# Rest q and k loaded for four heads per transfer set instead of two, with the load, transpose and v order of the second batch rearranged

## The chip, the cores and the metric

The kernel runs on one core of one Trainium2 chip. The metric is the device time of one execution in microseconds (us), lower is better. A core has five engines that run their own instruction streams and meet at semaphores: TensorE (PE, matmuls, with a separate row PEld for its weight loads), VectorE (DVE), ScalarE (ACT), GpSimd (POOL) and SyncE (SP). SP computes nothing here: it issues DMA transfers, one after the other, in program order. POOL issues transfers too, between its own computations. A transfer runs on its own once it is issued, and the instruction that needs the data waits for its semaphore.

## What is computed

Eight batches of eight heads of causal attention with a forgetting gate, then a two-layer MLP over the 4,608 tokens:

```python
batch, n_heads, seq, head_dim = (8, 8, 576, 64)

scores = np.matmul(q, k.transpose(0, 1, 3, 2)) / np.sqrt(D)
cum = np.cumsum(np.log(np.clip(f, 0.0001, 1.0)), axis=-1)
scores = np.where(causal, -1e9, scores + cum[:, :, :, None] - cum[:, :, None, :])
attn = np.exp(scores - max); attn = attn / (attn.sum(-1) + 1e-9)
x = np.matmul(attn, v).transpose(0, 2, 1, 3).reshape(4608, 512)
h = x @ w_in            # 512 -> 2048
out = (h / (1 + np.exp(-h))) @ w_out   # 2048 -> 512
```

## The kernel before

**Tiling.** A head's 576 tokens are cut into a first block of 128, three "rest" blocks of 128 (tokens 128 to 511), and a tail of 64. The first blocks of all batches have a path of their own at the start of the program. The rest works in **units**: unit n is two heads of batch n // 4, and with p = n % 4 these are heads `head(p, 0)` and `head(p, 1)` (L149): 0 and 2 for p = 0, 1 and 3 for p = 1, 4 and 6 for p = 2, 5 and 7 for p = 3. So units 2m and 2m + 1 share heads 0 to 3 or 4 to 7. There are 32 units, in 16 pairs m.

**The life of a unit.** These steps of one unit are named throughout:

- `load_qk` (L152, transfers at L158): SP loads q and k of the rest blocks into the staging tiles `qf` and `kf`. One transfer for each of q and k and each of the two heads, four in all, of 96 KB each. Four staging buffers of each.
- `load_tails` (L165, L168): the tails of all eight heads of a batch, one transfer for q and one for k, 128 KB each.
- `cast_qk` (L394): POOL turns them into bf16 in the tile `qkb`: two casts of 128x384 (L399, for q and k) and one of 128x128 (L403, tails).
- `transposes` (L423, L427): SP issues one DMA transpose from `qkb` to `qkT`. There are three `qkT` buffers, so the transpose of unit n also waits until the scores of unit n - 3 are done.
- `scores` (L444, L459): PE multiplies from `qkT`, in three pieces c = 0, 1, 2; ACT takes the exponential (L463, L475), DVE masks.
- `load_v` (L174, L179): SP loads v of a batch, one transfer for each of the blocks c = 0 to 3 (256 KB, the last one 128 KB), into one buffer for each block. `convert_v` (L409, L413): POOL multiplies it by the decay weights into `vp`, the operand of the second attention product.
- `attend` (L490): PE multiplies the exponentials by `vp` (L506, L515), DVE divides. `back` (L531) transposes the result into the MLP's input: on PE for the first pairs, by two DMA transposes on SP (L538, L542) for pairs 4 to 14.

**The MLP** is cut into small pieces (`m1_chunk`, L567, L575, L576, and `m2_part`, L612, L622). They are laid between the attention steps by a planner: `fill` and `slot` (L698, L863) put about so many microseconds of MLP matmuls at a place, by a fixed cost for each piece. The planner knows nothing of transfers. The output's stores (L591) are issued by POOL at fixed places of its own stream.

**Order.** Every engine's instructions run in the order in which the program writes them. There is no scheduler: a place in the Python text is a place in the queue. Two places set the order of the loads:

- The start (L783 to L803): load units 0, 1 and 2, then cast and transpose them, with `load_v(0, ...)`, `load_qk(3)` and `load_tails(1)` between, then `convert_v(0, ...)`.
- `prepare(n)` (L839), called once for each unit while unit n's scores are under way: it loads unit n + 4, and casts and transposes unit n + 2. Below is the part that matters; `b, p = divmod(n, 4)`.

```python
        if n > 1 and n + 4 < NU:
            load_qk(n + 4)
        if 0 < n < NU - 2:
            cast_qk(n + 2)
            transposes(n + 2)
        if n <= 1:
            load_qk(n + 4)
        ...
        if p == (1 if b > 0 else 2):
            for c in range(NM):
                load_v(b + 1, c)
```

For each pair m the main loop (L872) writes scores of unit 2m, pieces 0 and 1; `prepare(2m)`; `back(m - 1)`; MLP; scores of 2m, piece 2, and of 2m + 1, piece 0; `prepare(2m + 1)`; MLP; the other scores; MLP; then both `attend`.

Of the kernel before, what the change touches and what calls it, by code (L numbers as in the profile page):

```python
# [10 lines left out]
FP32 = mybir.dt.float32  # L11
BF16 = mybir.dt.bfloat16
P = 128
# [5 lines left out]
def kernel(  # L19
# [12 lines left out]
    B, H, S, D = q.shape  # L32
# [4 lines left out]
    NP = H // 2  # L37
    SM = 512
    ST = S - SM
    NM = SM // P  # L40
    NR = NM - 1
# [3 lines left out]
    NU = B * NP  # L45
    NQ = NU // 2
# [10 lines left out]
    stage = ctx.enter_context(tc.tile_pool(name="stage", bufs=1))  # L57
# [91 lines left out]
    def head(p, i):  # L149
        return p // 2 * 4 + 2 * i + p % 2  # L150

    def load_qk(n):  # L152
        b, p = divmod(n, NP)
        ts = []
        for name, src in (("qf", q), ("kf", k)):
            t = stage.tile([P, NR, 2, D], FP32, name=name, tag=name, bufs=4)
            for i in range(2):
                nc.sync.dma_start(  # L158
                    out=t[:, :, i, :],
                    in_=src[b, head(p, i), P:SM, :].rearrange("(c p) d -> p c d", p=P),  # L160
                )
            ts.append(t)
        qst[n] = tuple(ts)

    def load_tails(b):  # L165
        t = stage.tile([P, H, D], FP32, name="qktf", tag="qktf", bufs=2)
        for i, src in enumerate((q, k)):
            nc.sync.dma_start(  # L168
                out=t[i * ST : (i + 1) * ST, :, :],
                in_=src[b, :, SM:S, :].rearrange("h s d -> s h d"),  # L170
            )
        tst[b] = t

    def load_v(b, c):  # L174
        if c == 0:
            vst[b] = []
        t = vfs[c]
        r = slice(0, P) if c < NR else slice(ST, P)
        nc.sync.dma_start(  # L179
            out=t[r, :, 0:D],  # L180
            in_=v[b, :, P + c * P : min(S, P + (c + 1) * P), :].rearrange("h p d -> p h d"),
        )
        vst[b].append(t)
# [36 lines left out]
    for i in range(2):  # L220
        for g in range(2):
            nc.vector.tensor_copy(
                out=sel[:, i, :].rearrange("p (u w r) -> p u w r", u=2, w=2)[:, g, :, :],
                in_=ident_bf[:, :].rearrange("p (r u i w) -> p u i w r", u=2, i=2, w=2)[
                    :, g, i, :, :
                ],
            )

    def keep_warm(n):
# [7 lines left out]
        out=f_sb[:, :], in0=f_sb[:, :], scalar1=1e-4, scalar2=1.0, op0=ALU.max, op1=ALU.min  # L237
# [101 lines left out]
    def convert_v0(b):  # L339
        nc.gpsimd.tensor_tensor(  # L340
            out=v0[b][:, :, :],
            in0=vf0.pop(b)[:, :, :],
            in1=w_bf[:, 0, b * H : (b + 1) * H, None].to_broadcast([P, H, D + 1]),
            op=ALU.mult,
        )
# [48 lines left out]
    def cast_qk(n):  # L394
        b, p = divmod(n, NP)
        t2 = conv.tile([P, NX, 2 * D], BF16, name="qkb", tag="qkb")
        for i, t in enumerate(qst.pop(n)):
            c0 = i * (NR + 1)
            nc.gpsimd.tensor_copy(  # L399
                out=t2[:, c0 : c0 + NR, :].rearrange("p c x -> p (c x)"),  # L400
                in_=t[:, :, :, :].rearrange("p c h d -> p (c h d)"),
            )
        nc.gpsimd.tensor_copy(  # L403
            out=t2[:, NR, :].rearrange("s (i d) -> s i d", i=2),
            in_=tst[b].rearrange("s (u i w) d -> s u w i d", u=2, w=2)[:, p // 2, p % 2, :, :],
        )
        qbf[n] = t2

    def convert_v(b, c):  # L409
        vbf[b] = vps[b % 2]  # L410
        r = slice(0, P) if c < NR else slice(ST, P)
        n = r.stop - r.start
        nc.gpsimd.tensor_tensor(  # L413
            out=vbf[b][r, c, :, :],
            in0=vst[b][c][r, :, :],
            in1=w_bf[r, c + 1, b * H : (b + 1) * H, None].to_broadcast([n, H, D + 1]),
            op=ALU.mult,
        )
# [4 lines left out]
    def transposes(n):  # L423
        src = qbf.pop(n)
        t = qktp.tile([P, NX, P], BF16, name="qkT", tag="qkT")
        qkT[n] = t[:, :, :].rearrange("p x c -> p (x c)")
        nc.sync.dma_start_transpose(  # L427
            out=t[:, :, :], in_=src[:, :, :].rearrange("p x c -> p (x c)")
        )
# [352 lines left out]
    load_v0(7)  # L782
    after(w_out_bf[0:1, 2 * NFC // WQ - 1, DM - 16 : DM])  # L783
    load_qk(0)
    load_tails(0)
    load_qk(1)
    load_qk(2)
    cast_qk(0)
    transposes(0)
    convert_v0(6)  # L790
    convert_v0(7)
    load_v(0, 0)
    load_v(0, 1)
    cast_qk(1)
    transposes(1)
    load_v(0, 2)
    load_v(0, 3)
    load_qk(3)
    cast_qk(2)
    transposes(2)  # L800
    load_tails(1)
# [37 lines left out]
    def prepare(n):  # L839

        b, p = divmod(n, NP)
        if n > 1 and n + 4 < NU:
            load_qk(n + 4)
        if 0 < n < NU - 2:
            cast_qk(n + 2)
            transposes(n + 2)
        if n <= 1:
            load_qk(n + 4)
        if b + 1 == B:
            return  # L850
        if p == 0 and b > 0:
            load_tails(b + 1)
        if p == (1 if b > 0 else 2):
            for c in range(NM):
                load_v(b + 1, c)
        if p >= 2:
            for c in range(2 * (p - 2), 2 * (p - 1)) if b > 0 else range(NM * (p - 2)):
                convert_v(b + 1, c)
# [13 lines left out]
    for m in range(NQ):  # L872
        n = 2 * m
        piece = 1.7 if m < 2 else 2.4
        scores(n, 0)
        scores(n, 1)
        prepare(n)
        if m > 0:
            back(m - 1)
            if m % 2 == 0:  # L880
                b = m // 2 - 1
                pending.append([2, [REST_OF[b]] + ([TAILS_OF[b][0]] if b == NM - 1 else [])])
        slot(piece, 1, 0)
        scores(n, 2)
        scores(n + 1, 0)
        prepare(n + 1)
        slot(piece, 1, 0)
        scores(n + 1, 1)
        scores(n + 1, 2)
        slot(piece, 1, 0)  # L890
        attend(n)
        attend(n + 1)
        slot(min(3.5, max(0.8, behind() - LAG)) if m > 1 else 0.8)
# [38 lines left out]
```

## Time and profile before

| | us |
|---|---|
| median of 10 runs (345.59 to 350.22) | 347.68 |
| the profiled execution | 347.87 |
| its span in the trace | 346.1 |
| TensorE busy | 336.6 |
| ScalarE busy | 217.1 |
| VectorE busy | 180.4 |
| GpSimd busy | 127.5 |
| transfers of qf and of kf, 64 each of 96 KB: median from issue to landing | 3.0 and 3.2 |
| transfers of vf by SP, 26 of 256 KB: the same | 4.8 |
| transposes to qkT, 32: the same | 4.0 |

The span is the stretch between the first and the last instruction on the core; the execution's own time is 1.77 us longer. "Busy" is the time in which an engine has an instruction under way. PE's matmuls overlap each other, so the mean duration of one is more than the step from one to the next. An engine's rows in the timeline give the start, the length, the engine, the line and operation, and in brackets how long the engine had been idle before and which event ended that idle time. Rows of SPq are issues: their length is how long SP was occupied with issuing, and the data land later.

### The profile page before, as it was taken

To read this page: it belongs to the slowest core of one execution; us is meant where nothing else is said; L and a number is where in the kernel's file an instruction comes from. 1 tells how busy PE (TensorE), PEld (TensorE's weight loads), DVE (VectorE), ACT (ScalarE), POOL (GpSimd) and SP (SyncE) were. 2 spreads that over 40 slices of the span, in tenths; PEclk is the share of its full clock that TensorE was granted. 3 is DMA by queue.
4 is the path that set the end of the run, shared out by engine and by line. 5 is a ranking of instruction groups with operands and counts; after the bars stand their busy time and mean duration, and the time that the engine had idled before them with its cause. 6 is when DMAs were issued, how large, how long until landed. Compare 5 with 4: busy or idle time off the path is not lost.

```text
span 346.1 us, 8894 instructions
## 1 busy us (share of the span) xinstructions
PE 336.6 (97%) x3567; PEld 199.4 (58%) x3567; DVE 180.4 (52%) x389; ACT 217.1 (63%) x401; POOL 127.5 (37%) x227
## 2 busy tenths in 40 slices
PE   8999999998899999999999999999999999999995
PEld 3654655666466566466555666656656565555654
DVE  4756736367167566446545545555655454344330
ACT  5866644886457857759558686685776844454431
POOL 8986226734545083065045108208320000001011
PEclk9999999999899999999999999999999999999999
DMA  8999999999999998999798799989622010001012
GB/s 154 196 186 219 192 182 148 245 207 179 202 215 194 155 209 170 158 226 171 131 233 152 146 184 171 179 168 207 135 67 73 5 60 35 30 31 62 30 50 73
DMA packets 141497, 50.44 MB, mean 146 GB/s; under 512 B 132368, under 2 KB 138768, under 8 KB 141456
## 3 DMA queue, kind: packets, MB, share of 16 engines
q1 hardware_dynamic: 131440, 32.70, 56.0%
q0 software_dynamic: 9856, 17.04, 21.2%
q8 instruction: 28, 0.46, 0.6%
q10 hardware_dynamic: 160, 0.13, 0.2%
q14 instruction: 13, 0.11, 0.1%
HBM read 36.85 MB, written 9.44 MB: 134 GB/s over the span
## 4 chain that ended last, share of the span: by engine, by line
PE 85%; DMA 7%; POOL 2%; SPq 2%; ACT 1%; DVE 1%; issue 1%; POOLq 0%
PE po L612 35%; PE hp L567 33%; PE sc L459 6%; PE dn L506 4%; PE dn L515 2%; DMA w_in_bf<-in_moe_w_in_dram 2%; DMA vf<-in_v_dram 2%; PE tp L285 1%; DMA qkb<-in_k_dram 1%; DMA qkT<-qkb 1%; SPq L427 1%; DMA kf<-in_k_dram 1%; DVE gt L576 1%; SPq L158 1%; POOL vf L140 1%
## 5 line engine op out<-in xcount | busy, mean ns | idle before, releaser
L576 DVE SCALAR_TENSOR_TENSOR gt<-th,hp 128x384 bf16<-128x384 bf16 (+2 forms) x208 | 105.7, 522 | 83.8 <-ACT th L575 79.8
L575 ACT ACTIVATE th<-hp 128x384 bf16<-128x384 f32 (+2 forms) x208 | 95.2, 478 | 84.7 <-PE hp L567 82.4
L612 PE MATMUL po<-w_out_bf,gt 128*128 128x512 bf16 (+1 forms) x592 | 146.1, 376 | 0.0
L567 PE MATMUL hp<-x,w_in_bf 128*128 128x384 bf16 (+2 forms) x704 | 128.5, 322 | 0.4 <-DMA w_in_bf<-in_moe_w_in_dram 0.3
L567 PEld LDWEIGHTS <-w_in_bf 128*128 128x128 bf16 x832 | 80.0, 98 | 57.0 <-issue 0.8
L591 POOL DMA_DIRECT2D out_dram<-osb x38 | 21.0, 552 | 171.0 <-ACT osb L622 126.3
L463 ACT ACTIVATE u<-sc 128x1024 bf16<-128x1024 f32 (+1 forms) x96 | 75.1, 821 | 12.2 <-PE sc L459 12.2
L612 PEld LDWEIGHTS <-gt 128*128 128x128 bf16 x592 | 53.5, 98 | 48.3 <-issue 3.3
L413 POOL TENSOR_TENSOR vp<-vf,w_bf 128x520 bf16<-128x520 f32 (+1 forms) x32 | 34.1, 1071 | 13.8 <-DMA vf<-in_v_dram 8.9
L622 ACT ACTIVATE osb<-po 128x512 f32<-128x512 f32 (+1 forms) x37 | 22.1, 596 | 19.7 <-PE po L612 19.7
L468 DVE TENSOR_TENSOR u<-u,tri 128x768 bf16<-128x768 bf16 x32 | 20.5, 642 | 23.1 <-ACT u L463 23.1
L459 PE MATMUL sc<-qkT 64*128 64x128 bf16 (+1 forms) x640 | 27.1, 208 | 3.2 <-DMA qkT<-qkb 3.1
L459 PEld LDWEIGHTS <-qkT 64*128 64x128 bf16 x640 | 18.5, 95 | 14.7 <-issue 9.9
L482 DVE TENSOR_TENSOR ut<-ut,trit 128x128 bf16<-128x128 bf16 x32 | 8.7, 272 | 33.3 <-ACT ut L475 32.8
L475 ACT ACTIVATE ut<-sc 128x640 bf16<-128x640 f32 x32 | 23.3, 727 | 0.0
L399 POOL CAST qkb<-qf 128x384 bf16<-128x384 f32 x32 | 16.9, 528 | 15.7 <-DMA qf<-in_q_dram 15.3
L506 PEld LDWEIGHTS <-u 128*128 128x128 bf16 x576 | 20.8, 97 | 2.6
L506 PE MATMUL dn<-vp,u 128*128 128x65 bf16 x384 | 21.8, 193 | 0.0
L524 DVE TENSOR_TENSOR xr<-dn,rec 128x448 bf16<-128x448 f32 x32 | 20.0, 625 | 1.1
L506 PE MATMUL dn<-v,u 128*128 128x65 bf16 x192 | 19.8, 193 | 0.0
L567 PE MATMUL hp<-xt,w_in_bf 128*128 128x256 bf16 x128 | 17.7, 273 | 0.0
L399 POOL CAST qkb<-kf 128x384 bf16<-128x384 f32 x32 | 16.7, 520 | 2.7 <-DMA kf<-in_k_dram 2.6
(68 smaller groups left out, 204.6 us busy)
## 6 DMA issues: line engine op xcount, KB each, us to landing
out_dram<-osb POOLq DMA_DIRECT2D x32, 256.0 KB, 3.4
vf<-in_v_dram SPq DMA_DIRECT2D x26, 256.0 KB, 4.8
qf<-in_q_dram SPq DMA_DIRECT2D x64, 96.0 KB, 3.0
kf<-in_k_dram SPq DMA_DIRECT2D x64, 96.0 KB, 3.2
w_in_bf<-in_moe_w_in_dram POOLq DMA_DIRECT2D x4, 512.0 KB, 7.6
w_out_bf<-in_moe_w_out_dram POOLq DMA_DIRECT2D x4, 512.0 KB, 9.5
vf<-in_v_dram POOLq DMA_DIRECT2D x6, 256.0 KB, 9.8
qkb<-in_q_dram POOLq DMA_DIRECT2D x8, 128.0 KB, 5.2
```

The costliest lines, as they stand in the source:

```text
L399: nc.gpsimd.tensor_copy(out=t2[:, c0 : c0 + NR, :].rearrange("p c x -> p (c x)"), in_=t[:, :, :, :].rearrange("p c h d -> p (c h d)"),)
L413: nc.gpsimd.tensor_tensor(out=vbf[b][r, c, :, :], in0=vst[b][c][r, :, :], in1=w_bf[r, c + 1, b * H : (b + 1) * H, None].to_broadcast([n, H ...
L459: nc.tensor.matmul(sc[:, i, o : o + q1 - q0], lhsT=kt, rhs=t[r, q0:q1], start=True, stop=True)
L463: nc.scalar.activation(out=u[:, :, c * SM : c * SM + w], in_=sc[:, :, 0:w], func=ACT.Exp, scale=scale)
L475: nc.scalar.activation(out=ut[:, :, 0:3:2, :].rearrange("p k i t -> p i k t"), in_=sc[:, :, T0 : T0 + (NM + 1) * ST].rearrange("p i (k t) ...
L506: nc.tensor.matmul(dn[:, i * NR + c - 1, :], lhsT=u[:, i, o : o + P], rhs=vals(kb, i), start=(kb == 0), stop=(kb == c),)
L567: nc.tensor.matmul(hp[:, :], lhsT=w_in_bf[:, cc, fc * P : (fc + 1) * P], rhs=xcols(g, cc), start=(cc == 0), stop=(cc == NCC - 1),)
L575: nc.scalar.activation(out=th[:, :], in_=hp[:, :], func=ACT.Tanh, scale=0.5)
L576: nc.vector.scalar_tensor_tensor(out=gt[:, fc, :], in0=th[:, :], scalar=1.0, in1=hp[:, :], op0=ALU.add, op1=ALU.mult,)
L591: q_.dma_start(out=dst, in_=src)
L612: nc.tensor.matmul(po[:, :], lhsT=gt[:, fc, tb * P : (tb + 1) * P], rhs=w_out_bf[:, fc, m0:m1], start=(fc == 0), stop=(fc == NFC - 1),)
L622: nc.scalar.activation(out=osb[:, :], in_=po[:, :], func=ACT.Copy, scale=0.5)
```

## The change

`load_qk(m)` now serves a pair of units. Its tiles hold four heads, `[128, 3, 4, 64]`, with two buffers of each in place of four half as large. There is one transfer for each of q and k and each of the three token blocks (six for two units, 128 KB each), where there was one for each tensor and head (four for one unit). `cast_qk` picks its two heads, which now lie two apart, out of the four. The calls are moved: at the start two pairs are loaded in place of four units; in `prepare` the load comes after the cast and the transpose, once in two units; for batch 1 the four v transfers are split two and two around the transpose of unit 5 (`prepare(2)` and `prepare(3)`), and the pair 3 is loaded behind them. On SP's queue 32 transfers are gone; the streams of PE, DVE, ACT and POOL have the same instructions in the same order, POOL's first two casts of each unit with a different read pattern.

```diff
-    def load_qk(n):
-        b, p = divmod(n, NP)
+    def load_qk(m):
+
+        b, h0 = m // 2, m % 2 * 4
         ts = []
         for name, src in (("qf", q), ("kf", k)):
-            t = stage.tile([P, NR, 2, D], FP32, name=name, tag=name, bufs=4)
-            for i in range(2):
+            t = stage.tile([P, NR, 4, D], FP32, name=name, tag=name, bufs=2)
+            for c in range(NR):
                 nc.sync.dma_start(
-                    out=t[:, :, i, :],
-                    in_=src[b, head(p, i), P:SM, :].rearrange("(c p) d -> p c d", p=P),
+                    out=t[:, c, :, :],
+                    in_=src[b, h0 : h0 + 4, P + c * P : 2 * P + c * P, :].rearrange(
+                        "h p d -> p h d"
+                    ),
                 )
             ts.append(t)
-        qst[n] = tuple(ts)
+        qst[m] = tuple(ts)
...
     def cast_qk(n):
         b, p = divmod(n, NP)
         t2 = conv.tile([P, NX, 2 * D], BF16, name="qkb", tag="qkb")
-        for i, t in enumerate(qst.pop(n)):
+        for i, t in enumerate(qst[n // 2]):
             c0 = i * (NR + 1)
             nc.gpsimd.tensor_copy(
-                out=t2[:, c0 : c0 + NR, :].rearrange("p c x -> p (c x)"),
-                in_=t[:, :, :, :].rearrange("p c h d -> p (c h d)"),
+                out=t2[:, c0 : c0 + NR, :].rearrange("p c (i d) -> p c i d", i=2),
+                in_=t[:, :, :, :].rearrange("p c (i w) d -> p c w i d", w=2)[:, :, p % 2, :, :],
             )
...
     load_qk(0)
     load_tails(0)
-    load_qk(1)
-    load_qk(2)
     cast_qk(0)
     transposes(0)
     convert_v0(6)
     convert_v0(7)
-    load_v(0, 0)
-    load_v(0, 1)
+    load_qk(1)
     cast_qk(1)
     transposes(1)
-    load_v(0, 2)
-    load_v(0, 3)
-    load_qk(3)
+    for c in range(NM):
+        load_v(0, c)
     cast_qk(2)
     transposes(2)
     load_tails(1)
...
     def prepare(n):
 
         b, p = divmod(n, NP)
-        if n > 1 and n + 4 < NU:
-            load_qk(n + 4)
         if 0 < n < NU - 2:
             cast_qk(n + 2)
             transposes(n + 2)
-        if n <= 1:
-            load_qk(n + 4)
+        if n == 0:
+            load_qk(2)
+        if n == 4:
+            load_qk(4)
+        if n > 4 and n % 2 == 1 and (n + 5) // 2 < NQ:
+            load_qk((n + 5) // 2)
         if b + 1 == B:
             return
         if p == 0 and b > 0:
             load_tails(b + 1)
-        if p == (1 if b > 0 else 2):
-            for c in range(NM):
+        if b == 0 and p >= 2 or b > 0 and p == 1:
+            for c in range(NM) if b > 0 else range(2 * (p - 2), 2 * (p - 1)):
                 load_v(b + 1, c)
+        if n == NP - 1:
+            load_qk(3)
```

## The prediction

> **What bounds the kernel now.** I read the busy table first: TensorE (PE) is busy for 336.6 us of 346.1, no other engine for two thirds of the span. So a change to loads, which adds and removes no matmul, can only pay or cost where PE waits. The page has no such row, so next came the list of PE's own waits by window, and its timeline around the longest:
>
> ```profile
> PE 336.6 (97%) x3567; PEld 199.4 (58%) x3567; DVE 180.4 (52%) x389; ACT 217.1 (63%) x401; POOL 127.5 (37%) x227
> ...
> PEclk9999999999899999999999999999999999999999
> ```
>
> ```profile
> 74.15 0.40 PE L459 MATMUL sc<-qkT 64*128 64x128 bf16 x8 [0.48 <-DMA qkT<-qkb]
> ```
>
> ```profile
> 84.70 0.28 PE L459 MATMUL sc<-qkT 64*128 64x64 bf16 x8
> 87.63 0.61 PE L459 MATMUL sc<-qkT 64*128 64x128 bf16 x8 [2.65 <-DMA qkT<-qkb]
> 88.17 1.89 PE L612 MATMUL po<-w_out_bf,gt 128*128 128x512 bf16 x4
> 89.85 0.87 PE L567 MATMUL hp<-x,w_in_bf 128*128 128x256 bf16 x4
> ```
>
> After 95 us PE's list of waits is empty up to 250 us. Behind its start, PE has only two waits of weight: 0.48 us for the transposed q and k of unit 3 and 2.65 us for those of unit 5. I write t0, t1, ... for the transposes (L427) by unit. The bracket is the idle time before the row. PEclk, the granted clock in 40 slices, has a single slice under 9: the eleventh, 86.5 to 95.2 us, where this wait is. The windows (stretch, length, busy us of PE, PEld, DVE, ACT, POOL, granted clock, DMA share, GB/s) show why:
>
> ```profile
> 80.00:85.00 5.00, 4.98 (x71) 3.37 (x67) 4.24 (x10) 3.71 (x7) 2.84 (x3) 1.00 1.39 216
> 85.00:87.60 2.60, 0.00 (x0) 0.00 (x0) 1.04 (x2) 1.00 (x3) 2.47 (x5) 0.88 1.28 232
> 87.60:90.40 2.80, 2.77 (x15) 1.36 (x16) 0.56 (x1) 1.33 (x2) 1.87 (x6) 0.50 1.42 224
> 90.40:95.00 4.60, 4.60 (x39) 2.40 (x38) 0.65 (x2) 2.87 (x6) 1.49 (x3) 1.00 0.69 176
> ```
>
> The wait costs twice. After about 2 us of idleness the clock fell to 0.50 and stayed there 2.8 us beyond the restart; four 128x512 matmuls took 1.89 us, in the timeline's other rows of four 1.03. Half of 2.8 is **1.4 us** more. In all 0.48 + 2.65 + 1.4 = **4.5 us** hang on t3 and t5.
>
> Why was t5 late? SP's queue:
>
> ```profile
> 75.72 1.22 SPq L427 DMA_TRANSPOSE qkT<-qkb  x1
> 76.98 4.57 SPq L179 DMA_DIRECT2D vf<-in_v_dram  x4
> 81.60 1.15 SPq L158 DMA_DIRECT2D qf<-in_q_dram  x2
> 82.79 1.02 SPq L158 DMA_DIRECT2D kf<-in_k_dram  x2
> 83.92 1.25 SPq L427 DMA_TRANSPOSE qkT<-qkb  x1
> ```
>
> ```profile
> 76.59 0.29 POOL L403 CAST qkb<-qktf 128x128 bf16<-128x128 f32 x1
> ```
>
> Its input was cast at 76.88, but four v transfers and the four of load_qk(7) stood ahead of it, 7.0 us. (The chain of waits names POOL's vp at 83.14 as releaser; that is a coincidence of times: POOL's row shows the cast done long before.)
>
> **The change, part by part.**
> 1. *Fewer, larger transfers.* 128 transfers of 96 KB (four per unit, 384 pieces of 256 B each) become 96 of 128 KB (six per two units, 512 pieces). Bytes and pieces stay. SP issues one in 0.49 us with an empty queue (1.02 for x2), a 512-piece tail transfer (L168) in 0.62. I take 0.6 for the new form (bounds 0.5, 1.0): 128 x 0.51 = 65 us against 96 x 0.6 = 58 us of SP time. PE waits for none of it after 95 us, so it is worth 0 there; t8 to t31 landed 5 to 10 us ahead of their use (t8: issued 103.14, landed 3.8 us later; its scores' exponential is at 112.86). [...] The trace's landings are long too (qf 3.0 us), but several are in flight at once, and behind PE. [...]
> 2. *t5 moves up.* After: t4, two v, t5, two v, load_qk(3) (6), t6. Ahead of t5 stand two transfers (1.2 to 2.7 us by L179) instead of eight. Even with t4 a little late this puts t5 at about 76.5, landing about 80.5, against a need at 84.5 (87.63 less 3.13 of waiting). **-2.65 - 1.4.** The later queue has qk loads always behind the odd transpose, and once a batch six qk and four v in a row where it had four and four: +1.5 us before the next transpose, against 5 us or more of slack.
> 3. *The start gets heavier.* cast_qk(0) now needs 768 KB of q and k and 256 KB of tails where it needed 384 and 256. Before, these first transfers crawled beside the weights (qf issued 36.94, landed 46.2 and 48.3), then ran free: k landed by 49.7, tails 50.85, the second unit's four by 51.9, that is 640 KB in 2.2 us. The new first 1024 KB are the very bytes that had landed by 51.9; I take 52.2, cast done 52.5, t0 at 52.6. Before, the cast ended at 51.3, but t0 stood behind load_qk(2) until 52.31. So only +0.3; landing 3 to 4 us later meets its scores at 60.77.
> 4. *t1* now stands behind six transfers: 52.6 + 1.3 + 6 x 0.64 = 57.8 (was 55.41). Landings range from 3.0 to 5.9 us: 60.8 to 63.7, need 63.1. Hidden, just.
> 5. *v of batch 0* goes from 53.76 (two) and 57.77 (two) to 59.1. In the burst at 76.98 the last of four conversions (L413) ended 9.6 us after the first v's issue; with the faster first landing of 53.76 it is 8.7. So 67.8 to 68.7; attend(0) needs the fourth block at 68.8 (was done at 64.86). Just hidden.
> 6. *Then what is late next: t3.* Behind those conversions POOL has three stores and the cast of unit 3:
>
> ```profile
> 64.80 1.69 POOL L591 DMA_DIRECT2D out_dram<-osb  x3
> 66.54 0.50 POOL L399 CAST qkb<-qf 128x384 bf16<-128x384 f32 x1
> ```
>
> 68.3 + 1.7 + 1.25 = 71.3 for t3 (was 67.75, but then in a crowded queue: 2.97 us to issue, 6.4 to land, 74.15). load_qk(2) ahead of it is issued by 68.5, so its queue is quiet: landing 3.1 to 3.9, at 74.4 to 75.2, against a need of 73.67. **+1.2 us** of waiting in place of 0.48. SP behind it: t4 at about 73.8, landing by 78, need 80.8; osb's fifth buffer needs the first store back by 72.7 (68.3 + 3.7 = 72.0).
> 7. *The cast's form* (six pieces of 64 with gaps, not one run of 384) is not in the trace. The near row is L403, two gapped pieces of 64, 0.29 us; three of those are 0.87, one run is 0.51. I take 0.55, since L403 fits a fixed part plus length; at 0.87 t3 is 0.7 us later.
>
> Waits on one PE queue don't add up: the latest one shifts all that follows. So after: 1.2 us lost instead of 4.5, **-3.3**: 347.87 (the profiled execution, span 346.1) gives 344.6. The median of the runs shown is 347.68, 0.19 lower: **344.4**.
>
> Whether 1.2 us of waiting also costs clock: [...] the trace shows the fall after 2.0 us. By the row, waits up to 2 us are free (0.48 was); beyond I add 1.4. [...]
>
> **Rivals.**
> - *The new wait is long enough for the clock.* If t3 lands after about 76.3 (casts at 0.87, v conversions 0.7 late), 2.6 us + 1.4 = 4.0 stand for the old 4.5: 347.2. For it: every slack in steps 4 to 6 is under 1 us. Against: t3's quiet queue. 0.17.
> - *Slower: the four-head pattern drains slowly.* Pieces of one partition now lie in four heads, as in v. Lone first landings are 2.4 us for 96 KB of q and 3.6 for 256 KB of v: 160 KB in 1.2 us, 133 KB/us, against 290 in step 3. 768 KB then take 5.8 us; cast 0 is 2.5 us later, the next load 2 more, t3 lands at 79.4: a wait of 5.7 + 1.4 - 4.5 = +2.6: 350.3. It decides from a loss of 3.6 us ahead of t3 (landing 78.5). Against: v's burst at 76.98 brought 896 KB in 8.2 us with latency, about 190 KB/us. 0.17.
> - *It doesn't do what it says:* t5 stays late because the two v ahead of it block (up to 1.83 us each) and POOL casts unit 5 behind a late load_qk(2). It would have to move 8 us. 347.7. 0.06.
>
> **The numbers.** The forecast, 0.60: 343.2 (no new wait) to 345.7 (wait of 2.4 without clock). The range 342.9 to 347.8 adds most of the first and third rival and leaves out the slow pattern. A measurement here tells about 0.5% (1.7 us) from no change. Faster 0.60; same 0.21 (second and part of the first); slower 0.19 (the slow pattern and the worst of the first).
>
> **What would show it.** Right: no PE wait at unit 5, PEclk 9 in every slice, t5 issued near 76 to 77, a wait of about 1 us before unit 3's scores with t3 issued straight after its cast, POOL's fourth L413 ending near 68. Wrong: PE waits before units 0 or 1 or in attend(0), a cast above 0.6 us, six loads issued in over 5 us, waits after 95 us.

## The result and the profile after

| | before | after |
|---|---|---|
| median, us | 347.32 (344.94 to 350.22, 49 runs) | 349.64 (348.12 to 350.95, 14 runs) |
| ratio to before, 95% interval | | 1.0071 (1.0049 to 1.0094) |
| profiled execution, its span | 347.87, 346.1 | 350.95, 349.1 |
| PE busy | 336.6 | 338.5 |

The change costs 2.3 us. The forecast was 344.4, and the range ended at 347.8. The profiled execution of after is the longest of its 14 runs, so its sums stand about 1.3 us above its median. The medians take all runs; the ratios leave out those more than 1.5% above the fastest of their kernel, five of 22 in e12, one in e6 and four of before's beside the experiments.

Each run also has its granted clock, averaged over the execution. The 3.4 us at half clock that before's profile shows take 0.005 off it (that run has 0.995), the 6.8 us in after's, below, twice that (0.99). By that measure an execution of before loses at least one such stretch about every other time: 104 of the 185 that were run beside the experiments have 0.995 or less, with a median of 348.0 us, the other 81 have 345.9. Of after all 14 have 0.995 or less, eight of them 0.995 and three 0.99. Where in the execution the stretch lies only a profile can tell.

The busy row and the clock row of the page after:

```profile
PE 338.5 (97%) x3567; PEld 200.1 (57%) x3567; DVE 181.9 (52%) x389; ACT 217.4 (62%) x401; POOL 128.2 (37%) x227
...
PEclk9999999996999999999999999999999999999999
```

The same matmuls take 1.9 us longer, and the slow slice is now the tenth (78.5 to 87.3 us), with a 6 where before had an 8 in its eleventh. PE's timeline there; the first row ends unit 2's scores, the second begins unit 3's:

```profile
74.69 0.28 PE L462 MATMUL sc<-qkT 64*128 64x64 bf16 x8
78.23 0.61 PE L462 MATMUL sc<-qkT 64*128 64x128 bf16 x8 [3.26 <-DMA qkT<-qkb]
78.77 1.89 PE L615 MATMUL po<-w_out_bf,gt 128*128 128x512 bf16 x4
...
91.79 0.51 PE L462 MATMUL sc<-qkT 64*128 64x64 bf16 x16
```

Before, these rows had a wait of 0.48 us at unit 3 and 2.65 us at unit 5. Now it is 3.26 us at unit 3, and unit 5 has none: the last row joins the end of unit 4's scores and the start of unit 5's. Behind that restart four 128x512 matmuls take 1.89 us, as they did behind the old wait. How long the half clock lasts, from PE's windows (stretch, length, busy us of PE, PEld, DVE, ACT, POOL, granted clock, DMA share, GB/s):

```profile
77.00:77.50 0.50, 0.00 (x0) 0.00 (x0) 0.16 (x1) 0.00 (x0) 0.32 (x2) 1.00 0.97 190
77.50:78.00 0.50, 0.00 (x0) 0.00 (x0) 0.00 (x0) 0.00 (x0) 0.00 (x0) 0.51 1.11 217
...
83.50:84.00 0.50, 0.50 (x2) 0.15 (x1) 0.00 (x0) 0.50 (x2) 0.03 (x1) 0.50 1.16 202
84.00:84.50 0.50, 0.50 (x3) 0.24 (x2) 0.00 (x0) 0.50 (x2) 0.00 (x0) 0.66 1.27 220
```

From 77.5 to 84.3 the clock is 0.50. Of that, 6.1 us lie behind the restart at 78.23, at half pace: about 3 us more.

To see where the time came from I set each unit's scores against before (by the first matmul of 384 columns of each unit, which opens their second piece, in both profiled executions). The delay is +1.3 us for units 0 to 2, +6.0 at unit 3, +6.9 at unit 4, and +3.0 from unit 5 to the end, where it no longer moves. So:

- **+1.3 us ahead of unit 0.** PE waits 1.2 us for POOL's `v` of the first blocks (L343), where before it waited 0.2. Most of that, 0.9, lies in the opening, before the change does anything; over the profiles of this study the start differs by up to 2.2 us. The other 0.4 are two first-block conversions, `convert_v0(6)` and `(7)`, behind a late `cast_qk(0)` on POOL.
- **+4.7 and +0.9 at units 3 and 4.** 2.8 us of waiting more than before, and 2.8 us of half clock.
- **-3.9 at unit 5.** The wait and the slow clock that are gone.

SP's queue shows what is behind the new wait. These are issues; their length is SP's time:

```profile
48.77 0.64 SPq L171 DMA_DIRECT2D qktf<-in_k_dram  x1
54.02 1.34 SPq L430 DMA_TRANSPOSE qkT<-qkb  x1
55.41 1.70 SPq L159 DMA_DIRECT2D qf<-in_q_dram  x3
57.16 2.34 SPq L159 DMA_DIRECT2D kf<-in_k_dram  x3
59.60 1.35 SPq L430 DMA_TRANSPOSE qkT<-qkb  x1
61.05 3.63 SPq L182 DMA_DIRECT2D vf<-in_v_dram  x4
...
67.68 1.72 SPq L159 DMA_DIRECT2D qf<-in_q_dram  x3
69.45 1.60 SPq L159 DMA_DIRECT2D kf<-in_k_dram  x3
72.90 4.52 SPq L430 DMA_TRANSPOSE qkT<-qkb  x2
77.47 1.24 SPq L182 DMA_DIRECT2D vf<-in_v_dram  x2
78.82 2.10 SPq L430 DMA_TRANSPOSE qkT<-qkb  x1
```

From 49.4 to 54.0 SP issues nothing: t0 stands at the head of the queue, waiting for a cast that waits for the last of the first 1024 KB, and the next load is behind t0. The last row is t5, issued at 78.8 with scores at 91.8. The windows of before, then of after, over the stretch in which SP stands:

```profile
50.00:52.00 2.00, 2.00 (x25) 1.08 (x22) 0.66 (x1) 1.72 (x3) 1.31 (x3) 1.00 0.71 161
52.00:54.00 2.00, 2.00 (x13) 1.09 (x12) 2.00 (x3) 1.37 (x3) 2.00 (x3) 1.00 0.83 183
54.00:56.00 2.00, 2.00 (x27) 1.39 (x25) 1.93 (x7) 0.38 (x1) 1.91 (x5) 1.00 0.72 150
```

```profile
50.00:52.00 2.00, 2.00 (x25) 1.00 (x24) 0.34 (x2) 1.10 (x2) 0.41 (x1) 1.00 0.53 106
52.00:54.00 2.00, 2.00 (x13) 1.08 (x11) 1.67 (x3) 1.61 (x3) 1.09 (x3) 1.00 0.04 9
54.00:56.00 2.00, 1.72 (x17) 0.94 (x15) 0.86 (x3) 0.43 (x2) 2.00 (x3) 1.00 0.35 70
```

The last column is the one to read: 9 GB/s where 183 were moved. Over 46 to 58 us after moves 1.50 MB and before 2.07; the missing 0.57 MB are 3 us at the rate of before's windows. The depth of the hole differs from execution to execution: in e4, which has the same start, the windows from 50 to 54 us move 59 and 102 GB/s, and t0 is issued at 51.72. PE is nearly full in both stretches, so a list of PE's waits shows nothing here. The row of the DMA engines' busy tenths, whose seventh digit is 52.4 to 61.1 us, has the hole in one figure, first before, then after:

```profile
DMA  8999999999999998999798799989622010001012
```

```profile
DMA  8999995999598799999988869959832101001012
```

### The profile page after: what moved, and what is told of

Same layout as the page of the kernel before. It is cut to its first block, busy times and chain, and to the rows that moved or that the text cites. A ratio compares the mean times of both kernels' runs of the same rounds, so it can differ in the third digit from the quotient of the medians.

```text
span 349.1 us, 8836 instructions
## 1 busy us (share of the span) xinstructions
PE 338.5 (97%) x3567; PEld 200.1 (57%) x3567; DVE 181.9 (52%) x389; ACT 217.4 (62%) x401; POOL 128.2 (37%) x227
## 4 chain that ended last, share of the span: by engine, by line
PE 80%; DMA 9%; SPq 3%; POOL 3%; DVE 1%; ACT 1%; issue 1%; POOLq 0%
PE po L615 34%; PE hp L570 29%; PE sc L462 7%; PE dn L509 5%; DMA w_out_bf<-in_moe_w_out_dram 3%; SPq L159 3%; PE dn L518 3%; DMA w_in_bf<-in_moe_w_in_dram 2%; DMA vf<-in_v_dram 2%; DMA qkT<-qkb 2%; PE wm L235 1%; DMA qktf<-in_k_dram 1%; ACT u L466 1%; POOL v L343 1%; SPq L171 0%
## 5 line engine op out<-in xcount | busy, mean ns | idle before, releaser
L471 DVE TENSOR_TENSOR u<-u,tri 128x768 bf16<-128x768 bf16 x32 | 22.0, 688 | 22.9 <-ACT u L466 22.9
L485 DVE TENSOR_TENSOR ut<-ut,trit 128x128 bf16<-128x128 bf16 x32 | 9.4, 295 | 32.2 <-ACT ut L478 31.7
```

Source lines behind the costliest of these rows:

```text
L471: nc.vector.tensor_tensor(out=x, in0=x, in1=tri[:, None, None, :].to_broadcast([P, 2, NR, P]), op=ALU.mult,)
```

## The experiments

The theory after the result was that the order at the start is what costs, and that the move of t5 is a gain that this cost hides. The rivals: the block-wise form itself drains slowly (C, the second rival of the prediction); t3 is late because its cast comes late on POOL, against which D says that t3's landing is set by what is ahead of it in the queues; and the half clock is as large a part as the wait. Medians of before beside these runs were 346.7 to 347.4 us, so a difference of medians between two sets of runs is uncertain by some tenths; the ratios are each taken against the before of the same set. Each heading says from which kernel the edit starts.

### e1: only the move of t5, in before

```diff
-        if n > 1 and n + 4 < NU:
+        late = n <= 1 or n == 3
+        if not late and n + 4 < NU:
             load_qk(n + 4)
...
-        if p == (1 if b > 0 else 2):
-            for c in range(NM):
+        if b == 0 and p >= 2 or b > 0 and p == 1:
+            for c in range(NM) if b > 0 else range(2 * (p - 2), 2 * (p - 1)):
                 load_v(b + 1, c)
+        if n == 3:
+            load_qk(n + 4)
```

> The kernel before with only the last part of the change: loads by two heads as before, but the four v transfers of batch 1 split around the transpose of unit 5, and the load of unit 7 put behind them. Theory A (the late part of the change is a gain, the loss comes wholly from the heavier start): the wait of 2.65 us before the scores of unit 5 and its half clock (1.4 us) go, the wait for unit 3 stays near 0.5 us: about 343.3 us against 347.3. Rival B (a gain here only shows another wait next, so nothing is won): within 1 us of 347.3.

Measured: 344.88 us, 0.9955 (0.9923 to 0.9987). No wait at unit 5, and none at unit 3 either (PE comes there later, since the opening of this execution is 2.2 us longer than that of before's); the only scores that wait are unit 9's, for 0.6 us. The part is a gain, but of 1.6 us by the ratio and 1.9 by the medians, and not 4. The clock is part of it: 12 of its 15 runs have a granted clock above 0.995.

### e2: the second pair's load ahead of the first cast, in after

```diff
     load_tails(0)
+    load_qk(1)
     cast_qk(0)
     transposes(0)
     convert_v0(6)
     convert_v0(7)
-    load_qk(1)
```

> The changed kernel with one call moved: the second pair's load stands ahead of the cast and transpose of unit 0 on SP's queue instead of behind them. Theory A (the start loses because SP waits for the first cast with nothing in flight, DMA share 0.04 in 52 to 54 us, and everything behind is 2 to 3 us later): v is issued near 58.5 instead of 61.0, its fourth conversion ends near 67.5 instead of 70.0, the transpose of unit 3 lands near 74.5 to 75, PE's wait for it falls from 3.3 to below 0.7 us and the clock stays whole: 343.5 to 345 us. Rival C (transfers of four heads drain more slowly than those of two): the wait stays above 2 us, 348 us or more.

Measured: 346.22 us, 0.9972 (0.9953 to 0.9991): 3.4 us better than after (the difference of the medians) for one moved line, and a mean clock of 0.997 or more in all 22 runs. The same windows, and unit 3's wait:

```profile
50.00:52.00 2.00, 2.00 (x25) 1.08 (x22) 0.64 (x2) 1.70 (x3) 0.51 (x1) 1.00 0.70 156
52.00:54.00 2.00, 2.00 (x13) 1.12 (x12) 1.83 (x3) 1.39 (x3) 1.76 (x3) 1.00 1.01 226
54.00:56.00 2.00, 1.85 (x25) 1.23 (x24) 1.80 (x7) 0.38 (x1) 2.00 (x4) 1.00 1.12 200
```

```profile
74.82 0.40 PE L462 MATMUL sc<-qkT 64*128 64x128 bf16 x8 [0.86 <-DMA qkT<-qkb]
```

226 GB/s where after moved 9; the wait is 0.86 us for 3.26, and the clock row holds a 9 in every slice. v of batch 0 is issued 3.1 us earlier (57.97 for 61.05; e4, with after's start, has 59.12).

### e3: unit 3 cast early, in after

```diff
     cast_qk(2)
+    cast_qk(3)
     transposes(2)
...
         if 0 < n < NU - 2:
-            cast_qk(n + 2)
+            if n > 1:
+                cast_qk(n + 2)
             transposes(n + 2)
```

> The changed kernel with one cast moved: unit 3 is cast on GpSimd right behind unit 2, ahead of the four v conversions and the three stores. Theory A (unit 3's transpose is late because its cast stands behind v's conversions and the stores): its issue moves from 72.9 to the end of the loads ahead of it on SP, near 71.1, the wait falls from 3.3 to about 1 us and the clock stays whole: about 345 us. Rival D (the transpose is late because the queue is full of the pair-2 load and stores when it is issued, landing 5.3 us later instead of 3 to 4): it lands hardly earlier, wait above 2 us, 348 us or more.

Measured: 350.42 us, 1.0081 (1.0058 to 1.0104): no gain. SP's issue of t3 (with t4), and what PE then does:

```profile
71.06 8.62 SPq L430 DMA_TRANSPOSE qkT<-qkb  x2
```

```profile
78.40 0.40 PE L462 MATMUL sc<-qkT 64*128 64x128 bf16 x8 [3.35 <-DMA qkT<-qkb]
```

t3 was issued 1.8 us earlier and landed no earlier, 7.3 us later: it came behind pair 2's six loads, in the same queue. So the cast is not what makes t3 late; theory D held. What I had not expected is that this wait of 3.35 us left the clock at 1.00, while 3.26 us in after brought 6.8 us of half clock. That is the exception: 18 of the 20 runs of e3 have 0.995 or less. In the profiled execution the gain that the clock should have brought went into new waits of 0.7 and 1.25 us at units 7 and 8.

### e4: unused matmuls in the place of the wait, in after

```diff
         scores(n, 2)
+        if m == 1:
+            keep_warm(13)
         scores(n + 1, 0)
```

> The changed kernel with 13 matmuls of 128x512 on a zero tile (2.8 us at full clock, they compute nothing that is used) put on PE just ahead of the scores of unit 3, into the wait. Theory E (the wait costs a second time through the halved clock): granted clock 1.0 throughout, the wait itself no longer, 1.4 to 2.8 us less: 347 to 348.2 us against 349.6. Rival (the lower clock costs nothing by itself, since other work limits there): 349.6 or more.

Measured: 348.04 us, 1.003 (1.0009 to 1.005), better than after by 1.6 us by the medians and 1.4 by the ratios; the two intervals just touch. PE, then SP:

```profile
73.95 2.98 PE L235 MATMUL wm<-warm 128*128 128x512 bf16 x13
...
77.20 1.04 PE L615 MATMUL po<-w_out_bf,gt 128*128 128x512 bf16 x4
```

```profile
51.72 1.33 SPq L430 DMA_TRANSPOSE qkT<-qkb  x1
...
56.57 2.44 SPq L430 DMA_TRANSPOSE qkT<-qkb  x1
...
71.11 4.63 SPq L430 DMA_TRANSPOSE qkT<-qkb  x2
```

The unused matmuls fill the wait, and the four behind them take 1.04 us and not 1.89. PE does 3 us of nothing useful and the kernel is faster, and 21 of its 22 runs have a granted clock above 0.995, where none of after's has: the half clock costs after at least 1.4 to 1.6 us. Up to 73.9 us this kernel is after itself, so it shows after's start a second time, in an execution whose first cast came 2.3 us earlier (t0 at 51.72 for 54.02): t3 is issued at 71.11, lands 5.3 us later at 76.4, and would have kept PE waiting 2.4 us (unit 2's scores end at 74.02). The late t3 is not a matter of the profiled execution's late start.

### e5: the old form in the new places, in after

```diff
-            for c in range(NR):
+            for i in range(4):
                 nc.sync.dma_start(
-                    out=t[:, c, :, :],
-                    in_=src[b, h0 : h0 + 4, P + c * P : 2 * P + c * P, :].rearrange(
-                        "h p d -> p h d"
-                    ),
+                    out=t[:, :, i, :],
+                    in_=src[b, h0 + i, P:SM, :].rearrange("(c p) d -> p c d", p=P),
                 )
```

> The changed kernel with the same four-head tiles, the same places of the loads and the same casts, but one transfer for each tensor and head (eight of 96 KB for two units, the form of the kernel before) instead of one for each tensor and token block (six of 128 KB). Rival C (the form of the transfers slows them): 2 us or more faster than the changed kernel, towards 347. Theory A (place and amount of the loads decide, not their form): within 1 us of 349.6, PE's wait for unit 3 about 3 us or a little more, since SP has 32 issues more.

Measured: 351.56 us, 1.0134 (1.0095 to 1.0174): 1.9 us slower than after by the medians. Six transfers of four heads are better than eight of one head, by 1.9 us at these places, over six runs and with intervals that only just clear each other. The slow pattern of the prediction's second rival is refuted (C), but A's "within 1 us" missed too. In the profiles the form costs nothing at the start: from unit 2 to unit 5 e5 loses 1.65 us against before and after 1.68. The rest comes at units 8 and 14.

### e6 and e7: t3 ahead of pair 2's load, in after

e7 has e3's early cast, and this; e6 has e2's moved line besides.

```diff
-        if n == 0:
+        if n == 1:
             load_qk(2)
```

> The changed kernel with three moves: the second pair's load ahead of the first cast, unit 3's cast right behind unit 2's, and the transpose of unit 3 ahead of the third pair's load on SP's queue. Theory A with D (unit 3's transpose lands late because the third pair's six transfers are in the queue ahead of it): it is issued near 65, lands by 69, PE has no wait of over 0.3 us behind its start, 344 to 345 us. If the third pair's load, now about 2 us later, is the next to be late: a wait of up to 1.5 us before unit 4, 345 to 346.5.

> The changed kernel with unit 3's cast right behind unit 2's and the transpose of unit 3 ahead of the third pair's load on SP's queue; the second pair's load stays where the change put it. Theory D (the queue ahead of it makes unit 3's transpose late): it lands by 71 and the 3.3 us wait is gone; v and the conversions are as late as in the changed kernel, which costs below 0.5 us; the third pair's load comes 2 us later and unit 4 may wait up to 1 us: 345 to 347 us. If only the late first cast counts (A without D): 348.5 or more.

Measured: e6 347.81 us, 1.0033 (1.0012 to 1.0055); e7 348.85 us, 1.0059 (1.0033 to 1.0084). In both the wait at unit 3 is gone: with pair 2's loads behind it and not ahead, t3 landed in 3.6 us (e6) and 3.5 us (e7). It comes back at unit 7, and in e6 at unit 8 as well (0.92 us); e7, then e6:

```profile
102.73 0.61 PE L462 MATMUL sc<-qkT 64*128 64x128 bf16 x8 [3.00 <-DMA qkT<-qkb]
```

```profile
101.84 0.40 PE L462 MATMUL sc<-qkT 64*128 64x128 bf16 x8 [1.36 <-DMA qkT<-qkb]
```

Pair 2's load now starts later, and all loads behind it. e6 is some 2 us worse than e2 (1.0033 against 0.9972), which it was meant to improve, and above the 346.5 us at which its expectation ended. e7's time lies where it was expected if D were wrong, and its interval overlaps after's; but the trace shows what D said of t3, and the gain lost again at unit 7. Here a transpose that is moved forward puts another back.

### e8: e1 with t3 ahead of the load of unit 4, in before

```diff
-        if n <= 1:
-            load_qk(n + 4)
+        if n == 1:
+            load_qk(4)
+            load_qk(5)
```

> The kernel before with the v transfers of batch 1 split around the transpose of unit 5 (as in the first experiment) and, besides, the transpose of unit 3 ahead of the load of unit 4 on SP's queue. Theory D: no wait of PE for q and k at all, 0.5 us less than the first experiment: 344.4 us. If unit 4's load, now later, is the next to be late: a wait of about 1 us before unit 4, 345 to 346 us.

Measured: 345.22 us, 0.9947 (0.9925 to 0.9968), the same as e1 within the intervals. t3 landed in 4.3 us. No scores wait for a transpose at all; instead PE waits 1.4 us near unit 14 for the MLP's input (`x<-xr`, one of the transposes of `back`).

### e9: only the hole, in before

```diff
     load_tails(0)
-    load_qk(1)
-    load_qk(2)
     cast_qk(0)
     transposes(0)
+    load_qk(1)
+    load_qk(2)
```

> The kernel before with one edit: the loads of units 1 and 2 stand behind the transpose of unit 0 on SP's queue, as the changed kernel places its second load; sizes, buffers and the late part are those of before. Theory A (what the start loses is the time in which nothing is in flight while SP waits for the first cast, and it isn't made up for later): DMA share near 0 for some 2 us before that transpose, the wait for unit 5 grows from 2.65 us by 1.5 to 3 us, about 349 to 350.5 us. Rival F (the place is harmless, it is the amount that the first cast needs which costs): within 1 us of 347.3.

Measured: 349.31 us, 1.0064 (1.0025 to 1.0103), 2.3 us more, with the transfers and tiles of before. One of the two windows that have the hole (the one ahead of it, 48 to 50 us, moves 24 GB/s where before moved 124):

```profile
50.00:52.00 2.00, 2.00 (x25) 1.07 (x24) 0.33 (x2) 1.38 (x3) 2.00 (x3) 1.00 0.31 62
```

The wait at unit 3 is 1.51 us where it was 0.48; the one at unit 5, which was expected to grow, stays (2.50 us). The profiled executions of before and e9 are 1.4 us apart, so that these waits show only part of the 2.3 us. The place of the load alone makes a loss as large as that of the whole change.

### e11 and e12: how much the first cast waits for, and where the next load stands, in after

e12 loads units 0 and 1 by head, as before, into the new tiles: the four heads' transfers of unit 0, the tails, then those of unit 1, so that `cast_qk(0)` again needs 384 KB and the tails; pair 1 stays behind t0. In e11 `load_qk(1)` stands ahead of `cast_qk(0)` too, and v of batch 0 is split around t1 as before.

```diff
+    def load_first(w):
...
+        for t, src in zip(qst[0], (q, k)):
+            for i in (w, w + 2):
+                nc.sync.dma_start(
+                    out=t[:, :, i, :],
+                    in_=src[0, i, P:SM, :].rearrange("(c p) d -> p c d", p=P),
+                )
...
-    load_qk(0)
+    load_first(0)
     load_tails(0)
+    load_first(1)
+    load_qk(1)
     cast_qk(0)
```

(The last added line but one is in both, the last in e11 alone.)

> A version meant to beat both: the changed kernel, but units 0 and 1 are loaded by head in the order of before (so the first cast needs 384 KB again), the second pair's load stands ahead of the first cast, and v of batch 0 stands around the transpose of unit 1 as before; the six-transfer loads from pair 1 on and the split v of batch 1 stay. Theory A: start as in the kernel before, late part as in the changed one, 8 issues fewer in a batch on SP than the first experiment has in two: 344 to 345 us, PE's wait for unit 3 below 0.8 us, none for unit 5. If the four-head loads of pairs 2 and 3 are late by their size alone: a wait before unit 3, 4 or 7 of 1 to 2 us, 345.5 to 347 us.

> The changed kernel, but the four heads of units 0 and 1 are loaded by head in the order of before: unit 0's two heads, the tails, then unit 1's, so the first cast needs 384 KB of q and k in place of 768; the second pair's load stays behind the transpose of unit 0. It splits what the start lost into amount and place. If the place of the second load is all (theory A), the first cast is done near 51.5 instead of 54.0, but SP still waits for it with little in flight: 348 to 349.3 us. If the amount is most of it (rival F): 346.5 or less.

Measured: e11 345.11 us, 0.9943 (0.9923 to 0.9963); e12 347.63 us, 0.9985 (0.9955 to 1.0014). e11 has 229 GB/s in the window of the hole, no wait for a transpose and a 9 in every slice of the clock, and it beats before and after. But it is no better than e1 (0.9955), which keeps before's transfers throughout: with the start repaired, the larger transfers show no gain over the one moved group of v. e12 is 2.0 us better than after by the medians and lies between the two expectations, because its executions fall into two groups: 13 of 22 with a granted clock above 0.995, median 345.8 us, and nine with 0.995 or less, median 349.0. Its profiled execution is one of the nine: PE waits 3.05 us at unit 3, with a half clock behind it. Place alone (e2) brings 3.4 us, amount alone (e12) 2.0, both (e11) 4.5: less than their sum. That a smaller first amount shortens the hole and an earlier load fills it, so that it can be won only once, is argued: e12's t0 is issued at 52.27, earlier than in after (54.02) and later than in e4 (51.72). What e11's split of v adds was not tried by itself.

### e13: unused matmuls in the place of before's wait

```diff
         scores(n, 2)
+        if m == 2:
+            keep_warm(10)
         scores(n + 1, 0)
```

> The kernel before with ten unused matmuls of 128x512 (2.2 us) on PE just ahead of the scores of unit 5, into the wait of 2.65 us. Theory E (the halved clock behind that wait costs up to 1.4 us, in those executions in which the clock falls): granted clock 1.0 throughout, 0.5 to 1.4 us less, 346 to 346.8 us. Rival (it costs nothing by itself): within 0.3 us of 347.3 or more.

Measured: 347.51 us, 1.0013 (0.999 to 1.0037). A miss: no gain. In its trace the clock row holds a 9 in every slice but the last and unit 5 comes 0.9 us earlier than in before's, but the median does not move. The clocks of the single runs say why. The unused matmuls do keep the clock up: 19 of 22 runs have more than 0.995, of the 43 of before beside them 19. But those 19 take 347.4 us in the median where before's 19 take 345.8. In the executions whose clock would have stayed up the 2.2 us of matmuls cost about what they save in the others (before's other 24: 348.3 us).

## Why the prediction was wrong, point by point

**Right.** t5 no longer waits (step 2): e1 by itself is faster. The cast costs 0.53 us in the mean of 32 in both kernels (step 7, 0.55 taken). Nothing behind unit 5 costs anything: the delay is constant from there to the end. And what is late next is t3 (step 6), and as the first rival had it, with the half clock behind its wait (0.50 from 77.5 to 84.3 us).

**The step that failed: 6, the landing of t3.** The prediction says "so its queue is quiet: landing 3.1 to 3.9". It landed 5.3 us after its issue in after and in e4, 5.6 in e2, 7.3 in e3; ahead of pair 2's loads it landed in 3.6 and 3.5 (e6, e7). The queue was not quiet: in after pair 2's six loads were landing until 75.3 us and the three stores that POOL issues just ahead of t3's cast until 76.6. (Which of the two weighs more the runs don't separate.) In e4 the six loads were issued by 68.75, as forecast, and t3 still took 5.3 us. I had the near row in hand, before's own t3 with 6.4 us, and set it aside as crowded because load_qk(2) would be "issued by 68.5"; but issued is not landed. By that row step 6 gives 71.3 + 6.4 = 77.7, a wait of 4.0 us, and with 1.4 of clock 5.4 us against the 4.5 gone: slower. The second term of the same step, nothing for the clock, followed from the first: waits of 1.36 us (e6) and 1.51 us (e9) left the clock whole in their traces, this one costs 1.4 to 1.6 us (e4).

**The steps that were right in number and missed the cause: 3 to 5.** In e4 their times hold within 1.3 us: t0 at 51.72 (52.6 forecast), t1 at 56.57 (57.8), the last conversion of v ended at 68.2 (67.8 to 68.7), t3 at 71.11 (71.3). In after's own profile everything is 1.4 to 1.8 us later, from its later first cast on (t0 at 54.02); 0.9 of that is the late opening. Units 0, 1 and 2 wait for no transpose in either. But each step asked whether one event meets its own deadline, and took the DMA engines to be free to catch up. None asked what they have to do while t0 stands at the head of SP's queue: nothing, and in a stream that has a 9 in every slice from 9 to 130 us in before, that is not made up. So the forecast moved t3's issue from 67.75 to 71.3 and took it as given. e2 (3.4 us back for one line), e9 (2.3 us lost by place alone) and e11 (all of it repaired) show that this order is the loss; e12 shows that the amount the first cast waits for has a part in it.

**Step 2's size.** Of the 4.05 us (2.65 + 1.4) taken for t5, 1.6 to 1.9 are there (e1). The 1.4 us of half clock were read off one execution, and before loses the clock in about every other one (104 of 185). So no more than about half of that term belonged in the sum.

**Step 1.** "Worth 0" did not hold in the new order: it argued from the trace of before, in which nothing waits after 95 us, and left open what the old form would do in the new order. There it has waits that after has not, 0.9 us at unit 8 (115 us) and 1.3 us for the MLP's input (`x<-xr`), and is 1.9 us slower (e5).

**The rivals.** The second had the sign right and the wrong cause: the block form is faster, not slower. The chain that it drew behind that, a later cast 0, a later next load, t3 as the wait, is what happened, and t3's landing in after's profile (78.2) is close to its deciding point (78.5), which is a coincidence: in e4 it is 76.4. The first rival's case, t3 after 76.3 with the clock lost, came true as well, but its sum of 347.2 set 4.0 us against a gain of 4.5, and e1 shows no more than 1.9.

**The sum.** In the profiled executions: -0.48 -2.65 -1.4 as taken, +3.26 for t3 where 1.2 was taken, +2.8 of half clock where 0 was, +0.4 for first-block conversions that were not in it: +1.9, and with 0.9 of the opening, which is not the change's, 2.8 of the 3.1 us between them. On the medians: -1.9 for t5 (e1), +1.9 for t3 (2.4 us in e4's profile in place of 0.5), +1.6 for the clock (e4): +1.6 of the 2.3 us measured. The other 0.7 is not accounted for; the clock's 1.6 is a lower bound.

## What to carry to other kernels

When the order of a transfer queue changes, check not only that each transfer meets its deadline, but whether the DMA engines ever run dry: here a transpose at the head of SP's queue waited for data with the next load behind it, the engines moved 9 GB/s for 2 us, and nothing later made that up: the place cost 2.3 us (e9), and the next load put ahead of the transpose gave back 3.4 (e2). So put the next load ahead of an instruction that waits at the head of the queue. The bigger transfer set made the first consumer wait for 1024 KB where it had been 640; load the first set in small pieces and in the order of use, which brought 2.0 us here (e12). One late transfer moved forward made another late in e6 and e7 (waits of 1.36 and 3.00 us at unit 7) and hardly in e1 and e8 (0.57 us at unit 9, and no wait of scores at all), so look at what is behind it in the queue. And a profile is one execution: before a cost that it shows goes into a sum, look at the other runs, here at their clocks, to see how often it occurs.

## What the runs showed of the hardware

**The half clock lasted 3.4 us, or twice that.** Read from half-microsecond windows, the stretches at 0.50 ran from 87.0 to 90.4 us in before, 88.95 to 92.36 in e9, 102.3 to 105.7 in e7 and 77.0 to 80.4 in e5: 3.4 us each, and 6.8 us, twice that, in after. The waits ahead of them were 2.65, 2.50, 3.00, 3.51 and 3.26 us; 3.35 us in e3's profile had none. In e12 PE's timeline shows it behind 3.05 us: four 128x512 matmuls took 1.89 us at 77.32 and 1.04 at 81.04. So neither the occurrence nor the length follows the wait's length. In before the clock fell 2.0 us after the wait began, in after 2.5, in e5 3.2: the 2 us up to which the prediction took waits to be free were an estimate from one wait. What sets the start and the length of a stretch was not shown.

**Transposes landed later behind loads in flight.** t0 in after, with next to nothing in flight (9 GB/s), landed in 3.0 us (54.0 to 57.0); t3 in 5.3 us, behind six loads of its queue and three stores from POOL; in e3, right behind the six loads, in 7.3 us; ahead of them, in e6 and e7, in 3.6 and 3.5. The issue took longer too: t3 in e3 occupied SP for 3.9 us, t0 in after for 1.3.
